# Gated linear attention plus a squared-ReLU MLP on one core: the first four chunks of x and w1 are loaded, split and multiplied in another arrangement

## The chip, the cores and the metric

One NeuronCore of a Trainium2 chip runs the whole kernel in one launch. The metric is device time in microseconds (us), the median over several runs; lower is better. One further execution was recorded by the hardware profiler, and every duration below comes from that recording.

## The reference

For x of 2048 x 448 the reference computes linear attention (branch a) and an MLP (branch b), mixed by a gate g for each row. It is cut to its core here:

```
x = A_x                                              # 1 x 2048 x 448
g = sigmoid((x * gate_w).sum(-1, keepdims=True))
# a: 16 heads of 28; phi(t) = where(t > 0, t + 1, exp(t)) + 1e-6
kv = einsum("bhsd,bhse->bhde", phi(k), v);  z = sum over s of phi(k)
a  = (phi(q) @ kv / (phi(q) . z + 1e-6)) @ wo
# b: 448 -> 1792 -> 448
h  = x @ w1 + b1
b  = relu(h)**2 @ w2 + b2
out = g * a + (1 - g) * b
```

All data are float32. The kernel keeps that precision by splitting each operand into a "hi" part, rounded to the format that TensorE multiplies (fp32r), and a "lo" part, the rest. A product is then three matmuls: hi by hi, lo of x by hi of w, hi of x by lo of w.

## The kernel before

The 2048 rows of x are four blocks of 512 columns of the transposed x (TB = 512). The 448 features are four chunks c of 128 partitions: chunks 0 to 2 are full, and chunk 3 holds the last 64 features twice, so that one matmul there does two of the three products. The 1792 hidden units are 14 tiles f of 128; seven of them make a half.

The program is one long list in a hand-written order; the order of the instructions on TensorE (PE), ScalarE (ACT) and VectorE (DVE) is that of the code. Loads are issued by SyncE (SP) through `load`, also in that order; a few transfers are issued by GpSimd (POOL).

The change touches the program's start. TensorE first runs 14 matmuls on constants (`warm_ps`). SyncE loads chunk 0 of x and of w1 in two transfers `xw` of 128 x 512, each with one half of both (`xw_raw[0]`, `xw_raw[1]`, in the profile `xwr`), and then chunks 1 to 3, x and w1 in turn, as six transfers of 256 KB with rows of 2 KB (`xr` and `w1r`). Each lands in a slot of a pool of 15 slots that the whole kernel goes round.

The splits follow. For chunk 0, ScalarE makes the hi part of x (`xh`) and VectorE that of w1 (`w`) for each half; TensorE multiplies the first two hidden tiles in halves of 256 columns (line 548), and VectorE makes the lo parts of x (`xl`), then of w1. For chunks 1 to 3, ScalarE makes hi of x, then hi of w1, and VectorE lo of x, then lo of w1 (`split_x`, `split_w1`, with `split_hi` on line 65 or 69, `split_lo` on line 72, and for chunk 3 of x `split_last` on lines 77 and 78). TensorE's matmuls of `up_chunk` (line 229) go term by term over the four tiles in chunk 0:

```
        if c == 0:
            for n in range(3):
                for f in range(0 if n else 2, 4):
                    up_chunk(first[f], 0, f, c, n)
        else:
            for f in range(4):
                up_chunk(first[f], 0, f, c)
```

In chunks 1 to 3 all three terms of one tile stand together, then those of the next. After chunk 3 come the keys of the first rows (`k_ps`, line 254), which need the split of `wk`, and the down product of tile 0 (`o_ps`, line 254), which needs `hh` and `hl`, the split of tile 0's squared ReLU (`hidden`). From there on the kernel goes in the same manner through all blocks.

Two further places matter. `hmask` is loaded into `hmr` by GpSimd in block 2 and split by ScalarE into `hm`. `queries` exchanges halves of 16 partitions for its chunk 3 (`swap`, line 475): four of the eight small transfers `qr<-qv` are issued by SyncE, four by GpSimd; VectorE adds the result in `join` (line 479).

Of the kernel before, what the change touches and what calls it, by code (L numbers as in the profile page):

```python
# [7 lines left out]
F = mybir.dt.float32  # L8
# [5 lines left out]
S, D, FF, H = 2048, 448, 1792, 16  # L14
DH = D // H
P = 128
TB = 512
NB = S // TB
NT = S // P
# [8 lines left out]


@with_exitstack  # L30
def gated_mix_kernel(ctx: ExitStack, tc: tile.TileContext, xw, xt, xn, wk, wq, wv, wo, w1a, w1b, w2, b1, b2, gw,
                     hmask, kvmask, halves, out):
    nc = tc.nc
    act, dve, pool, pe, sp = nc.scalar, nc.vector, nc.gpsimd, nc.tensor, nc.sync

    keep = ctx.enter_context(tc.tile_pool(name="keep", bufs=1))
# [11 lines left out]
    def bank(name):  # L48
        turn[0] ^= 1
        return ms_p.tile([P, 512], F, name=name, tag=f"ms{turn[0]}")  # L50
# [6 lines left out]
    def load(dst, src):  # L57
        sp.dma_start(out=dst, in_=src)  # L58
# [4 lines left out]
    def split_hi(eng, hi, src):  # L63
        if eng is act:
            act.activation(hi, src, AF.Copy)  # L65
        elif eng is pool:
            pool.tensor_scalar(hi, src, 1.0, 0.0, op0=ALU.mult, op1=ALU.add)
        else:
            eng.tensor_copy(hi, src)  # L69

    def split_lo(eng, lo, src, hi):
        eng.tensor_tensor(lo, src, f32(hi), op=ALU.subtract)  # L72
# [29 lines left out]
    x_raw, xs = {}, {}  # L102

    def load_x(b, c):
        x_raw[b, c] = slot([P, TB], F, f"xr{b}_{c}")
        load(x_raw[b, c], xt[b, c])
# [22 lines left out]
    w1_s, w1_raw = {}, {}  # L129

    def load_w1(h, g, c):
        w1_raw[h, g, c] = slot([P, (TB, 3 * P)[g]], F, f"w1r{h}{g}{c}")
        load(w1_raw[h, g, c], (w1a, w1b)[g][h, c])

    def new_w1(h, g):
        n, a, z = ((TB, 0, 16), (3 * P, 48, 0))[g]
        w = keep.tile([P, a + 7 * n + z], R, name=f"w1_{h}{g}", tag=f"w1{g}", bufs=1)
        w1_s[h, g] = w[:, a:a + 7 * n].rearrange("p (c n) -> p c n", c=7)
        return w1_s[h, g]
# [30 lines left out]
    ctx.enter_context(tc.manual_schedule(engines={pe.engine, act.engine, dve.engine}))  # L170


    part = [keep.tile([P, D], F, name=f"part{t}") for t in range(NT)]
    warm = nc.const_aps.tensor(1.0, (P, 256), mybir.dt.bfloat16)
    warm_ps = acc_p.tile([P, 512], F, name="warm_ps", tag="acc")
    for _ in range(14):
# [7 lines left out]
    xw_raw = []  # L184
    for n in range(2):
        xw_raw.append(slot([P, TB], F, f"xwr{n}"))
        load(xw_raw[n], xw[n])
    for c in range(1, 4):
        load_x(0, c)
        load_w1(0, 0, c)  # L190
    b1_s = keep.tile([P, NF], F, name="b1_s")
    half = keep.tile([P, 2], F, name="half")
    ones = keep.tile([P, 2], F, name="ones")
# [24 lines left out]
    def up_chunk(ps, b, f, c, only=None):  # L218
        h, fl = divmod(f, NH)
        g, i = divmod(fl, 4)  # L220
        w, cols = w1_s[h, g], slice(i * P, (i + 1) * P)
        xh, xl = xs[b]
        if c < 3:
            terms = [(w[:, c, cols], xh[:, c]), (w[:, c, cols], xl[:, c]), (w[:, 4 + c, cols], xh[:, c])]
        else:
            terms = [(w[:, 3, cols], xh[:, 3]), (w[:, 3, cols], xl[:, 3])]
        for n, (a, m) in enumerate(terms):
            if only in (None, n):
                pe.matmul(ps, a, m, start=(c == 0 and n == 0), stop=(c == 3 and n == 1))  # L229
# [219 lines left out]
    def queries(b, c):  # L449
        ps = bank(f"q_ps{b}_{c}")  # L450
        xh, xl = xs[b]
        cols = slice(c * P, (c + 1) * P)
        if c < 3:
            products(ps, terms_w(xh, xl, wq_s, cols))
        else:
            products(ps, [(wq_s[:, i, cols], x[:, i]) for i in range(4) for x in ((xh, xl) if i < 3 else (xh,))])
        e = slot([P, TB], F, f"qe{b}_{c}")
        r = slot([P, TB], F, f"qr{b}_{c}")
        v = slot([P, TB], F, f"qv{b}") if c == 3 else None
        pq[b, c] = e  # L460

        def after():
            phi(ps if c < 3 else v, e, r, e)
            if (b, "s") not in den:
                den[b, "s"] = slot([P, TB], F, f"ds{b}")
                dve.tensor_scalar(den[b, "s"], e, zc[:, c:c + 1], None, op0=ALU.mult)
            else:
                dve.scalar_tensor_tensor(den[b, "s"], e, zc[:, c:c + 1], den[b, "s"], op0=ALU.mult, op1=ALU.add)

        def swap():  # L470

            act.copy(v, ps)  # L472
            for p in range(0, P, 32):
                load(r[p:p + 16], v[p + 16:p + 32])
                pool.dma_start(out=r[p + 16:p + 32], in_=v[p:p + 16])  # L475
            return [join]

        def join():
            dve.tensor_tensor(v, v, r, op=ALU.add)
            after()  # L480
        return [swap if c == 3 else after]
# [53 lines left out]

    first = [mm_p.tile([P, 512], F, name=f"h_ps0_{f}", tag="mm") if f < 2 else bank(f"h_ps0_{f}") for f in range(4)]
    for c in range(4):
        if c == 0:  # L540
            xs[0] = new_x(0)
            w, (xh, xl) = new_w1(0, 0), [x[:, 0] for x in xs[0]]
            sides = slice(0, TB // 2), slice(TB // 2, TB)
            for n, cols in enumerate(sides):
                split_hi(act, xh[:, cols], xw_raw[n][:, sides[0]])
                split_hi(dve, w[:, 0, cols], xw_raw[n][:, sides[1]])
                for f in range(2):
                    pe.matmul(first[f][:, cols], w[:, 0, f * P:(f + 1) * P], xh[:, cols], start=(n == 0), stop=False)  # L548
            for m, (lo, hi) in enumerate(((xl, xh), (w[:, 4], w[:, 0]))):
                for n, cols in enumerate(sides):  # L550
                    split_lo(dve, lo[:, cols], xw_raw[n][:, sides[m]], hi[:, cols])
        else:
            split_x(0, c)
            split_w1(0, 0, c)
        if c == 0:
            for n in range(3):
                for f in range(0 if n else 2, 4):
                    up_chunk(first[f], 0, f, c, n)
        else:
            for f in range(4):  # L560
                up_chunk(first[f], 0, f, c)
    split_w2(0)
    split_w2(1)
    wk_s = keep.tile([P, 7, D], R, name="wk_s", tag="wkm", bufs=1)
# [53 lines left out]
    for b in range(1, NB):  # L618
        for f in range(NH):
            leave = leaves[b][f]  # L620
            run_todo()
            up(b, f)
            if f == 0:
                down(b - 1, NH - 1)
                half_done(b - 1)
                if b == 1:
                    for c in range(1, 4):
                        todo += gram(0, c)
                        run_todo()
            else:  # L630
                down(b, f - 1, leave=leave)
            if f == 1:
                todo += late_keys
                run_todo()
            if f == 0:
                load_xn(4 * b)
            if f < 4:
                if f < 3:
                    load_xn(4 * b + f + 1)
                if f == 0 and leave:  # L640
                    late_keys = keys(4 * b, leave)
                else:
                    late_keys = []
                    todo += keys(4 * b + f)
            elif f < 6:
                todo += gram(b, f - 4)
            else:
                todo += gram(b, 2)
                run_todo()
                todo += gram(b, 3)  # L650
            if b + 1 < NB:
                if 1 <= f < 5:
                    load_x(b + 1, f - 1)
                if 3 <= f:
                    split_x(b + 1, f - 3)
            if b == 2:
                if f < 4:
                    load_wq(f)
                if 1 <= f < 5:
                    split_wq(f - 1)  # L660
                if f == 5:
                    raw = slot([P, P], F, "hmr")
                    pool.dma_start(out=raw, in_=hmask)
                    split_hi(act, hm, raw)
                    load(half, halves)
            if b == 3:
                if f < 4:
                    load_w1(1, 0, f)
                if f == 4:
                    for c in range(4):  # L670
                        split_w1(1, 0, c)
                if f >= 2:
                    load_w2(NH + f - 2)
                if f >= 3:
                    split_w2(NH + f - 3)
                if f == 5:
                    key_sums()
                if f >= 5:
                    load_kv(2 * f - 10)
                    load_kv(2 * f - 9)  # L680
# [5 lines left out]
    for n, b in enumerate(order):  # L686
        then = order[n + 1] if n + 1 < NB else None
        for f in range(NF - NH, NF):
# [46 lines left out]
            if n == 0:  # L735
# [4 lines left out]
                if fl == 0:  # L740
                    for c in range(4):
                        load_w1(1, 1, c)
                    raw = kv_product()
# [29 lines left out]
    last, t = order[-1], 4 * order[-1] + 3  # L773
# [67 lines left out]
```

## Time and profile before

| | us |
|---|---|
| median of 3 runs (434.93 to 435.53) | 435.01 |
| the profiled execution's own time | 434.59 |
| its span, first to last instruction | 432.8 |
| TensorE busy | 428.8 |
| VectorE busy | 284.9 |
| ScalarE busy | 174.6 |
| GpSimd busy | 72.1 |

The span is what the profile's rows divide up; the remaining 1.8 us of the execution's own time lie around it. Matmuls are pipelined, so a busy TensorE can still lose time: how far apart the matmuls start says more than the busy share.

### The profile page before, as it was taken

To read this page: it belongs to the slowest core of one execution; us is meant where nothing else is said; L and a number is where in the kernel's file an instruction comes from. 1 tells how busy PE (TensorE), PEld (TensorE's weight loads), DVE (VectorE), ACT (ScalarE), POOL (GpSimd) and SP (SyncE) were. 2 spreads that over 40 slices of the span, in tenths; PEclk is the share of its full clock that TensorE was granted. 3 is DMA by queue.
4 is the path that set the end of the run, shared out by engine and by line. 5 is a ranking of instruction groups with operands and counts; after the bars stand their busy time and mean duration, and the time that the engine had idled before them with its cause. 6 is when DMAs were issued, how large, how long until landed. Compare 5 with 4: busy or idle time off the path is not lost.

```text
span 432.8 us, 5574 instructions
## 1 busy us (share of the span) xinstructions
PE 428.8 (99%) x2058; PEld 380.7 (88%) x2058; DVE 284.9 (66%) x464; ACT 174.6 (40%) x302; POOL 72.1 (17%) x93
## 2 busy tenths in 40 slices
PE   9999999999999999999999999999999999999997
PEld 6889999898989899898898888988888888888986
DVE  5999518843499437884459777887653966457624
ACT  6865324521346133453145543444433534233421
POOL 0055006500065002540010441000100001000000
PEclk9999999999999999999999999999999999999999
DMA  8742302020231211223234321230101401002002
GB/s 284 239 134 63 96 0 71 24 68 2 69 87 64 69 45 48 65 58 110 63 115 149 72 63 38 61 123 0 26 0 44 141 0 27 0 0 86 0 2 85
DMA packets 18412, 29.11 MB, mean 67 GB/s; under 512 B 2897, under 2 KB 12737, under 8 KB 18385
## 3 DMA queue, kind: packets, MB, share of 16 engines
q1 hardware_dynamic: 16480, 26.46, 19.8%
q0 software_dynamic: 1760, 2.20, 2.3%
q8 instruction: 16, 0.26, 0.3%
q14 instruction: 12, 0.09, 0.1%
q10 hardware_dynamic: 144, 0.10, 0.1%
HBM read 22.43 MB, written 3.67 MB: 60 GB/s over the span
## 4 chain that ended last, share of the span: by engine, by line
PE 98%; DMA 1%; ACT 0%; DVE 0%; SPq 0%; issue 0%
PE h_ps L229 32%; PE o_ps L254 31%; PE q_ps L84 8%; PE a_ps L84 8%; PE g_ps L84 8%; PE k_ps L254 8%; PE kv_ps L404 1%; DMA xwr<-in_xw 1%; PE m_ps L84 1%; PE d_ps L84 0%; PE last L84 0%; PE z_ps L398 0%; PE h_ps L548 0%; ACT xh L65 0%; DVE last L785 0%; SPq L58 0%
## 5 line engine op out<-in xcount | busy, mean ns | idle before, releaser
L254 PE MATMUL o_ps<-w,hh 128*128 128x448 f32 x444 | 127.8, 362 | 0.0
L229 PE MATMUL h_ps<-xh,w 128*128 128x512 f32 x390 | 124.6, 390 | 0.0
L254 PEld LDWEIGHTS o_ps<-w,hh 128*128 128x128 f32 x444 | 83.2, 188 | 7.6
L229 PE MATMUL h_ps<-xl,w 128*128 128x512 f32 x224 | 86.7, 389 | 0.0
L229 PEld LDWEIGHTS h_ps<-xh,w 128*128 128x128 f32 x390 | 73.1, 188 | 14.7 <-DVE w L72 0.4
L254 PE MATMUL o_ps<-w,hl 128*128 128x448 f32 x222 | 80.4, 362 | 0.0
L233 ACT ACTIVATE hr<-h_ps,b_s 128x512 f32<-128x512 f32 x56 | 38.1, 680 | 85.9 <-PE h_ps L229 80.6
L69 DVE CAST hh<-hr 128x512 fp32r<-128x512 f32 x56 | 23.6, 421 | 61.4 <-ACT hr L234 61.3
L229 PEld LDWEIGHTS h_ps<-xl,w 128*128 128x128 f32 x224 | 42.0, 188 | 7.9
L254 PEld LDWEIGHTS o_ps<-w,hl 128*128 128x128 f32 x222 | 41.6, 188 | 3.7
L72 DVE TENSOR_TENSOR hl<-hr,hh 128x512 fp32r<-128x512 f32 x56 | 39.7, 709 | 3.3
L72 POOL TENSOR_TENSOR nl<-xnr,nh 128x384 fp32r<-128x384 f32 x16 | 17.2, 1075 | 119.0 <-ACT nh L65 118.9
L234 ACT ACTIVATE hr<-hr 128x512 f32<-128x512 f32 x56 | 35.4, 632 | 1.8
L84 PE MATMUL q_ps<-xh,wq_s 128*128 128x512 f32 x100 | 33.0, 389 | 0.0
L84 PE MATMUL a_ps<-m_s,qh 128*128 128x448 f32 x112 | 32.7, 362 | 0.0
L254 PE MATMUL k_ps<-wk_s,xh 128*128 128x448 f32 x112 | 32.7, 361 | 0.0
L475 POOL DMA_DIRECT2D qr<-qv x16 | 7.9, 505 | 124.2 <-ACT qv L472 94.4
L72 DVE TENSOR_TENSOR pl<-r,ph 128x448 fp32r<-128x448 f32 x16 | 23.7, 1482 | 0.0
L326 POOL TENSOR_TENSOR ksum<-ksum,r 128x448 f32<-128x448 f32 x15 | 23.3, 1557 | 1.1 <-DVE r L288 1.1
L84 PE MATMUL q_ps<-xl,wq_s 128*128 128x512 f32 x60 | 23.3, 389 | 0.0
L254 PE MATMUL k_ps<-wk_s,xl 128*128 128x448 f32 x64 | 23.2, 363 | 0.0
L84 PE MATMUL a_ps<-m_s,ql 128*128 128x448 f32 x64 | 23.2, 362 | 0.0
(118 smaller groups left out, 571.0 us busy)
## 6 DMA issues: line engine op xcount, KB each, us to landing
xr<-in_xt SPq DMA_DIRECT2D x27, 256.0 KB, 2.7
xnr<-in_xn SPq DMA_DIRECT2D x16, 224.0 KB, 2.6
out<-out SPq DMA_DIRECT2D x15, 224.0 KB, 1.9
w2r<-in_w SPq DMA_DIRECT2D x14, 224.0 KB, 2.8
w1r<-in_w1a SPq DMA_DIRECT2D x7, 256.0 KB, 2.8
w1r<-in_w1b SPq DMA_DIRECT2D x8, 192.0 KB, 3.4
m_s<-m POOLq DMA_DIRECT2D x12, 112.0 KB, 2.5
wqr<-in_wq SPq DMA_DIRECT2D x4, 256.0 KB, 2.7
```

What stands on the lines that cost most here:

```text
L69: eng.tensor_copy(hi, src)
L72: eng.tensor_tensor(lo, src, f32(hi), op=ALU.subtract)
L84: pe.matmul(out_ps, a, b, start=(i == 0), stop=(i == n - 1))
L229: pe.matmul(ps, a, m, start=(c == 0 and n == 0), stop=(c == 3 and n == 1))
L233: act.activation(r, ps, AF.Relu, bias=b1_s[:, f:f + 1])
L234: act.activation(r, r, AF.Square)
L254: pe.matmul(ps, a, m, start=start, stop=stop)
L326: pool.tensor_tensor(ksum, ksum, p, op=ALU.add)
L404: pe.matmul(kv_ps[:JE, js], wv_s[c][:, js], gsum[c][:, js], start=(c == 0), stop=(c == 3))
L475: pool.dma_start(out=r[p + 16:p + 32], in_=v[p:p + 16])
```

## The change

1. Chunks 1 to 3 of x and of the first 512 columns of w1 stand side by side in one input `xw4`. Each chunk is one transfer of 512 KB with rows of 4 KB. It lands in `sums`, one tile that later serves as the 16 tiles `part`; the six pool slots are no longer taken.
2. Chunk 0: VectorE makes the hi part of x, ScalarE that of w1, in tiles of 128 columns.
3. Chunk 1: VectorE makes the hi part of x, ScalarE that of w1. Chunks 2 and 3 are split as before.
4. Chunk 1's matmuls go term by term over the four tiles, as chunk 0's do.
5. In block 0's exchange, two of GpSimd's four transfers go to SyncE; `hmask` is loaded by SyncE.

```diff
-    part = [keep.tile([P, D], F, name=f"part{t}") for t in range(NT)]
+    sums = keep.tile([P, NT * D], F, name="sums")
+    part = [sums[:, t * D:(t + 1) * D] for t in range(NT)]
...
     for c in range(1, 4):
-        load_x(0, c)
-        load_w1(0, 0, c)
+        raw = sums[:, 2 * TB * (c - 1):2 * TB * c]
+        load(raw, xw4[c - 1])
+        x_raw[0, c], w1_raw[0, 0, c] = raw[:, :TB], raw[:, TB:]
...
-                pool.dma_start(out=r[p + 16:p + 32], in_=v[p:p + 16])
+                (sp if b == 0 and p < 64 else pool).dma_start(out=r[p + 16:p + 32], in_=v[p:p + 16])
...
             for n, cols in enumerate(sides):
-                split_hi(act, xh[:, cols], xw_raw[n][:, sides[0]])
-                split_hi(dve, w[:, 0, cols], xw_raw[n][:, sides[1]])
+                split_hi(dve, xh[:, 0, cols], xw_raw[n][:, sides[0]])
                 for f in range(2):
-                    pe.matmul(first[f][:, cols], w[:, 0, f * P:(f + 1) * P], xh[:, cols], start=(n == 0), stop=False)
+                    split_hi(act, w[:, 0, (2 * n + f) * P:(2 * n + f + 1) * P], xw_raw[n][:, (2 + f) * P:(3 + f) * P])
+                for f in range(2):
+                    pe.matmul(first[f][:, cols], w[:, 0, f * P:(f + 1) * P], xh[:, 0, cols], start=(n == 0), stop=False)
...
+        elif c == 1:
+            split_hi(dve, xh[:, c], x_raw[0, c])
+            split_hi(act, w[:, c], w1_raw[0, 0, c])
+            split_lo(dve, xl[:, c], x_raw[0, c], xh[:, c])
+            split_lo(dve, w[:, 4 + c], w1_raw[0, 0, c], w[:, c])
         else:
             split_x(0, c)
             split_w1(0, 0, c)
-        if c == 0:
-            for n in range(3):
-                for f in range(0 if n else 2, 4):
-                    up_chunk(first[f], 0, f, c, n)
-        else:
-            for f in range(4):
-                up_chunk(first[f], 0, f, c)
+        for n in range(3) if c < 2 else (None,):
+            for f in range(2 if (c, n) == (0, 0) else 0, 4):
+                up_chunk(first[f], 0, f, c, n)
...
-                    pool.dma_start(out=raw, in_=hmask)
+                    load(raw, hmask)
```

How the order of instructions moves is read from the two built programs. On TensorE, at the first matmuls of chunk 1, there stands before (`h_ps_0` to `h_ps_3` are the four hidden tiles; `xh`, `xl` and `w` as above, where `w` holds both hi and lo of w1):

```order
L229 MATMUL h_ps_0_165<-xh_169,w_00_171 128x512
L229 MATMUL h_ps_0_165<-xl_170,w_00_171 128x512
L229 MATMUL h_ps_0_165<-xh_169,w_00_171 128x512
L229 MATMUL h_ps_1_166<-xh_169,w_00_171 128x512
L229 MATMUL h_ps_1_166<-xl_170,w_00_171 128x512
L229 MATMUL h_ps_1_166<-xh_169,w_00_171 128x512
```

In the changed program, the same place of TensorE reads:

```order
L232 MATMUL h_ps_0_141<-xh_145,w_00_147 128x512
L232 MATMUL h_ps_1_142<-xh_145,w_00_147 128x512
L232 MATMUL h_ps_2_143<-xh_145,w_00_147 128x512
L232 MATMUL h_ps_3_144<-xh_145,w_00_147 128x512
L232 MATMUL h_ps_0_141<-xl_146,w_00_147 128x512
L232 MATMUL h_ps_1_142<-xl_146,w_00_147 128x512
L232 MATMUL h_ps_2_143<-xl_146,w_00_147 128x512
L232 MATMUL h_ps_3_144<-xl_146,w_00_147 128x512
L232 MATMUL h_ps_0_141<-xh_145,w_00_147 128x512
```

The lo part of x is asked for four matmuls after the chunk's first one, no longer one, and the lo part of w1 eight, no longer two.

On ScalarE, its first splits stand so before:

```order
L65 ACTIVATE xh_169<-xwr_110 128x256
L65 ACTIVATE xh_169<-xwr_112 128x256
L65 ACTIVATE xh_169<-xr_1_114 128x512
L65 ACTIVATE w_00_171<-w1r_116 128x512
L65 ACTIVATE xh_169<-xr_2_118 128x512
L65 ACTIVATE w_00_171<-w1r_120 128x512
L77 ACTIVATE xl_170<-xr_3_122,side 128x512
```

On ScalarE in the changed program (`sums` holds the raw chunks):

```order
L65 ACTIVATE w_00_147<-xwr_95 128x128 x2
L65 ACTIVATE w_00_147<-xwr_97 128x128 x2
L65 ACTIVATE w_00_147<-sums 128x512
L65 ACTIVATE xh_145<-sums 128x512
L65 ACTIVATE w_00_147<-sums 128x512
L77 ACTIVATE xl_146<-sums,side 128x512
```

Two splits of 256 columns became four of 128, and the hi part of chunk 1 of x left ScalarE; it stands on VectorE now, ahead of that chunk's two lo parts.

## Rows read from the trace of the kernel before

**Rows 1.** The page: busy time by engine, and the chain that ended last.

```profile
PE 428.8 (99%) x2058; PEld 380.7 (88%) x2058; DVE 284.9 (66%) x464; ACT 174.6 (40%) x302; POOL 72.1 (17%) x93
...
PE 98%; DMA 1%; ACT 0%; DVE 0%; SPq 0%; issue 0%
```

**Rows 2.** Timeline of matmuls: start us, us, engine, line, operation, tiles, count.

```profile
3.99 1.11 PE L548 MATMUL h_ps<-xh,w 128*128 128x256 f32 x4
4.94 0.63 PE L229 MATMUL h_ps<-xh,w 128*128 128x512 f32 x2
...
7.58 0.40 PE L229 MATMUL h_ps<-xl,w 128*128 128x512 f32 x1
...
13.09 0.39 PE L229 MATMUL h_ps<-xh,w 128*128 128x512 f32 x1
...
14.91 0.57 PE L254 MATMUL k_ps<-wk_s,xh 128*128 128x448 f32 x2
```

**Rows 3.** Timeline of weight loads (PEld); in brackets idle time and its releaser.

```profile
4.59 0.30 PEld L548 LDWEIGHTS h_ps<-xh,w 128*128 128x128 f32 x2 [0.28 <-ACT xh L65]
...
7.24 0.19 PEld L229 LDWEIGHTS h_ps<-xh,w 128*128 128x128 f32 x1 [0.29 <-ACT w L65]
...
7.97 0.30 PEld L229 LDWEIGHTS h_ps<-xh,w 128*128 128x128 f32 x2 [0.43 <-DVE w L72]
```

**Rows 4.** Timeline of ScalarE, then of VectorE, at the start.

```profile
4.12 0.42 ACT L65 ACTIVATE xh<-xwr 128x256 fp32r<-128x256 f32 x1 [0.19 <-DMA xwr<-in_xw]
5.90 0.63 ACT L65 ACTIVATE xh<-xr 128x512 fp32r<-128x512 f32 x1 [1.36 <-DMA xr<-in_xt]
6.56 0.63 ACT L65 ACTIVATE w<-w1r 128x512 fp32r<-128x512 f32 x1
...
4.13 0.29 DVE L69 CAST w<-xwr 128x256 fp32r<-128x256 f32 x1 [0.31 <-DMA xwr<-in_xw]
4.33 0.75 DVE L72 TENSOR_TENSOR xl<-xwr,xh 128x256 fp32r<-128x256 f32 x2
5.00 0.76 DVE L72 TENSOR_TENSOR w<-xwr,w 128x256 fp32r<-128x256 f32 x2
```

**Rows 5.** Groups by line and shape, ScalarE and VectorE: count, busy us, mean ns.

```profile
L65 ACT ACTIVATE hm<-hmr 128x128 fp32r<-128x128 f32 x1 | 0.3, 296 | 0.0
...
L69 DVE CAST hh<-hr 128x512 fp32r<-128x512 f32 x4 | 1.7, 427 | 0.3 <-ACT hr L234 0.2
```

**Rows 6.** Windows: us, busy by engine (count), PEclk, DMA share, GB/s.

```profile
4.50:5.00 0.50, 0.43 (x4) 0.41 (x4) 0.50 (x2) 0.04 (x1) 0.00 (x0) 1.00 0.92 176
5.00:5.50 0.50, 0.50 (x4) 0.41 (x4) 0.50 (x3) 0.00 (x0) 0.00 (x0) 1.00 0.75 287
7.00:7.50 0.50, 0.50 (x3) 0.26 (x2) 0.50 (x2) 0.50 (x2) 0.00 (x0) 1.00 1.05 406
...
15.00:60.00 45.00, 45.00 (x221) 41.06 (x220) 33.26 (x54) 23.26 (x44) 12.43 (x12) 1.00 0.33 95
```

**Rows 7.** Timelines of VectorE and of weight loads at the first down product.

```profile
15.60 0.69 DVE L72 TENSOR_TENSOR hl<-hr,hh 128x512 fp32r<-128x512 f32 x1
...
17.32 0.19 PEld L254 LDWEIGHTS o_ps<-w,hl 128*128 128x128 f32 x1
```

**Rows 8.** The moved transfers: the queries on tiles hmr and qv, and timelines.

```profile
L663 POOL DMA_DIRECT2D hmr<-in_hmask x1: 704/704/704, 139.0 to 139.0; - x1
L65 ACT ACTIVATE hm<-hmr x1: 296/296/296, 146.1 to 146.1; 128x128 fp32r<-128x128 f32 x1
...
133.69 0.33 SPq L58 DMA_DIRECT2D xr<-in_xt  x1
...
252.67 3.72 SPq L58 DMA_DIRECT2D qr<-qv  x4
...
262.60 0.69 DVE L479 TENSOR_TENSOR qv<-qv,qr 128x512 f32<-128x512 f32 x1
DMA to landing us min/median/max: 2.7/3.8/4.5
```

More of the change, by code (lines that the diff above doesn't have):

```diff
@@ L30, in gated_mix_kernel @@
 @with_exitstack
-def gated_mix_kernel(ctx: ExitStack, tc: tile.TileContext, xw, xt, xn, wk, wq, wv, wo, w1a, w1b, w2, b1, b2, gw,
+def gated_mix_kernel(ctx: ExitStack, tc: tile.TileContext, xw, xw4, xt, xn, wk, wq, wv, wo, w1a, w1b, w2, b1, b2, gw,
                      hmask, kvmask, halves, out):
@@ L541, in gated_mix_kernel @@
             xs[0] = new_x(0)
-            w, (xh, xl) = new_w1(0, 0), [x[:, 0] for x in xs[0]]
+            w, (xh, xl) = new_w1(0, 0), xs[0]
             sides = slice(0, TB // 2), slice(TB // 2, TB)
             for n, cols in enumerate(sides):
-                split_hi(act, xh[:, cols], xw_raw[n][:, sides[0]])
-                split_hi(dve, w[:, 0, cols], xw_raw[n][:, sides[1]])
+                split_hi(dve, xh[:, 0, cols], xw_raw[n][:, sides[0]])
                 for f in range(2):
-                    pe.matmul(first[f][:, cols], w[:, 0, f * P:(f + 1) * P], xh[:, cols], start=(n == 0), stop=False)
-            for m, (lo, hi) in enumerate(((xl, xh), (w[:, 4], w[:, 0]))):
+                    split_hi(act, w[:, 0, (2 * n + f) * P:(2 * n + f + 1) * P], xw_raw[n][:, (2 + f) * P:(3 + f) * P])
+                for f in range(2):
+                    pe.matmul(first[f][:, cols], w[:, 0, f * P:(f + 1) * P], xh[:, 0, cols], start=(n == 0), stop=False)
+            for m, (lo, hi) in enumerate(((xl[:, 0], xh[:, 0]), (w[:, 4], w[:, 0]))):
                 for n, cols in enumerate(sides):
                     split_lo(dve, lo[:, cols], xw_raw[n][:, sides[m]], hi[:, cols])
+        elif c == 1:
[3 more added lines that the diff above has]
+            split_lo(dve, w[:, 4 + c], w1_raw[0, 0, c], w[:, c])
         else:
@@ L815 @@
                         for n in range(2)]),
+        "xw4": np.concatenate([xt[0, 1:], w1[0, 1:, :, :TB]], axis=2),
         "xt": xt,
```

## The prediction

> **What bounds the kernel.** I read the page of the profile first: TensorE is busy 428.8 us, and the chain of waits is 98% TensorE [rows 1]. Then the windows: from 15 to 60 us TensorE works 45.00 of 45.00 us, at the full granted clock of 1.00 (2.4 GHz) [rows 6]. So only the work ahead of about 15 us can be won, where the timelines of matmuls and weight loads show waits. Eight 512-column matmuls lie between the starts at 13.09 and 14.91: (14.91 - 13.09) / 8 = 0.2275 us each when nothing waits [rows 2]. From the start at 4.94 to the first `k_ps` at 14.91 there are 42 of them (10 of chunk 0, 12 + 12 + 8 of chunks 1 to 3), which need 9.56; they take 9.97. So **0.41 us is lost in waits** behind 4.94. The weight loads show where: at 7.24 for ScalarE's hi part of w1, at 7.97 for VectorE's lo part [rows 3], both in chunk 1; the rest are the restarts behind them. Ahead of 4.94 there is the wait at 4.59 for ScalarE's hi part of x [rows 3].
>
> **Chunk 0: hi parts on exchanged engines.** The second half of `xw` is there at 4.12. ScalarE made its x part in 0.42, to 4.54, and the weight load followed at 4.59, 0.05 later [rows 3, 4]. VectorE takes 0.29 for as many columns, from 4.13 to 4.42 [rows 4], so the matmul can start at 4.47, and those at 4.94 move to 4.82: **0.12 gained**. The first half gains as much and no longer decides. Cover: ScalarE now makes w1's tiles of 128 columns, a shape whose duration only another tile shows, 0.30 [rows 5]. The two tiles of the second half are ready by 4.12 + 0.30 + 0.30 = 4.72 at the latest, and the second is asked for at 4.82 + 0.23 = 5.05; if it took 0.42 as 256 columns do, 4.96, still in time. VectorE's four lo parts keep their times, since they follow two casts of 256 columns as before: xl ready at 5.08 and asked for at 5.28, w1's at 5.76 and asked for at 6.19 [rows 4]. Chunk 0's last matmul is then followed at 4.82 + 10 x 0.2275 = 7.10.
>
> **Chunk 1: one transfer, split on two engines, matmuls by terms.** Before, ScalarE made hi of x at 5.90 and hi of w1 behind it at 6.56, in 0.63 each [rows 4]; now it makes only w1's, while VectorE casts x in 0.43 [rows 5]. The first matmul can start 0.63 + 0.05 after the landing. VectorE's xl comes 0.43 + 0.69 + 0.05 = 1.17 after the landing (0.69 is a lo part of 512 columns [rows 7]) and is asked for four matmuls, 0.91, after the first, that is 1.59 after the landing at the earliest; w1's lo comes by 1.91 and is asked for at 2.50. So both waits behind the chunk's first matmul go, and their cover is at least 0.4. What is left is the first matmul. It loses nothing when the 512 KB have landed by 7.10 - 0.68 = 6.42, or by 6.2 if its weight load is to be as far ahead as usual.
>
> When they land is not shown, since no load of that form is in this trace. Lower bound: `xw` was there at 4.12, and 524 kB at 406 GB/s take 1.29 [rows 6], so 5.41. Upper bound: the same bytes were both there at 6.56 [rows 4]. Between them lies a slack of the queues of 176 and 287 GB/s from 4.50 to 5.50 [rows 6], whose cause the rows don't tell. I take the middle, about 6.0: seven tenths of the way from 5.41 to 6.56 lie below 6.2. Then all 0.41 is recovered. At the upper bound the first matmul starts at 7.24 as before and restarts with 0.11 lost (7.58 - 7.24 = 0.34 against 0.23 [rows 2, 3]): `k_ps` at 7.24 + 0.11 + 32 x 0.2275 = 14.63, a gain of 0.28 in all.
>
> The Trainium skill, DMA: Bandwidth & Descriptors, section Bandwidth, advises transfers of 1 MiB and gives 0.95 us for 64 KB and 6.15 us for 1 MB; read straight between these, my estimate is 2.0 for 256 KB and 3.4 for 512 KB. One transfer instead of two would by that save 0.6, so land at 5.96 and give the full 0.54. No run here shows that saving: parts of 256 KB landed 0.66 apart, which 406 GB/s fills without a pause [rows 4, 6].
>
> **Chunks 2 and 3.** They keep their order. At the latest they land 1.29 and 2.58 after the upper bound, 7.85 and 9.14. ScalarE's two hi parts of chunk 2 then end at 7.85 + 2 x 0.63 = 9.11, and TensorE asks for them at 7.10 + 12 x 0.2275 = 9.83; its lo of x is ready at 9.17 + 0.05 and its lo of w1 at about 9.9, asked for at 10.06 and 10.28. Chunk 3 takes one ScalarE step and three VectorE steps: 9.14 + 0.63 + 3 x 0.69 = 11.84, an estimate from these rows, against 12.56. No cost.
>
> **The rest.** The six pool slots set free let later loads go out sooner, and `sums` takes its part sums long after the raw chunks were split; TensorE waits for none of them, as its full window shows [rows 6]. `hmask` was issued at 139.0 and used at 146.1; SyncE's last issue ahead of it was at 133.69, so it is free, and a landing after 4.5, the longest that rows 8 show, still leaves 2.6 [rows 8]. In block 0's exchange SyncE issues six transfers in place of four from 252.67 on. Four took 3.72, so six end by about 3.72 x 6 / 4 = 5.6 later, at 258.3; with the longest landing of 4.5 counted from an issue's start, about 0.9 ahead of that end (3.72 / 4), the last is there by 261.9, and VectorE adds at 262.60 [rows 8]. Without that cover VectorE's queue would stand still, with the next hidden tile's split behind it. GpSimd saves two issues ahead of nothing that TensorE waits for. All this at zero.
>
> **Sum.** 0.12 + 0.41 = 0.53 to 0.54 gained. The profiled execution gives 434.59 - 0.54 = 434.05; it lies 0.42 under the median of the runs shown, so against that median I forecast 435.01 - 0.54, **434.5 us**. The gain reaches the end if nothing behind needs TensorE late. The nearest cover is tile 0's `hl`, ready at 15.60 + 0.69 = 16.29 and loaded at 17.32 [rows 7]: of 1.03 there stay 0.49.
>
> **Rivals.**
> - **The pair lands when its second part did.** The x part was usable at 5.90, 0.66 before the w1 part [rows 4]; one transfer makes x wait for both. For it: the slack of 4.50 to 5.50 would lie in the same place. Gain 0.28: 434.7. The Trainium skill, DMA: Bandwidth & Descriptors, section Why a DMA increments its semaphore by 16 and not by 1, says that only the full count, of all engines, tells that the data are there; the trace agrees in that ScalarE's start on each part came separately.
> - **The gain is returned at the first down product.** VectorE has one split of 0.43 more in chunk 1; if it and a late third transfer make VectorE more than 0.49 later at `hl`, TensorE waits there. Against: VectorE starts x itself and doesn't wait 0.63 for ScalarE. Price up to the whole 0.54: 435.0.
> - **Slower.** The transfer for chunk 1 lands late as a whole, because half of it meets the slack and nothing may start until the rest is there. From a landing at 6.84 the gain of 0.28 is gone, and every tenth behind that costs a tenth; from 7.71 the kernel is slower by 0.87, 435.9 or more. Against: no more bytes stand ahead of it than before.
> - **Faster than the sum.** If `xw` itself lands earlier, because less traffic stands behind it, TensorE's start moves as a whole. 0.33 of that with the 0.54 gives 434.1. Against: the two `xw` transfers and what is ahead of them don't change.
>
> **Chances.** About 0.2%, 0.87 us, is what a measurement of this kernel can tell from no change. The forecast has 0.58 (its own range 434.3 to 434.7), the late pair 0.20, the returned gain 0.06, slower 0.06, faster than the sum 0.10. The first three, 0.84, are within 0.2%; faster is 0.10 and slower 0.06. The range that should hold 8 in 10 goes from 434.0 to 435.3.
>
> **What would show it.** In the changed profile: the first weight load of the second half of chunk 0 at about 4.47; chunk 1's first matmul at 7.1 to 7.24; no weight load waiting for a lo part of w1; `k_ps` at 14.4 (14.6 in the first rival); `hl` loaded without a wait near 16.8; windows from 15 us on full. I am wrong if the first `k_ps` is later than 14.7, if TensorE waits behind 15 us, or if a matmul of chunk 2 or 3 waits for a landing.

## The result, and the profile after

The kernel lost 0.55 us: 435.51 us median (434.49 to 436.29, 22 runs) against 434.96 of the kernel before, measured beside it (22 runs), ratio 1.0013 with a 95% interval of 1.0007 to 1.0019. The forecast was 434.5, with a range of 434.0 to 435.3. The profiled execution took 435.55 us, its span 433.8.

The loss stands in one place. Timeline of the changed kernel's matmuls (columns as in [rows 2]; in brackets idle time and its releaser):

```profile
4.02 1.01 PE L553 MATMUL h_ps<-xh,w 128*128 128x256 f32 x4
4.87 0.63 PE L232 MATMUL h_ps<-xh,w 128*128 128x512 f32 x2
...
6.26 1.08 PE L232 MATMUL h_ps<-xh,w 128*128 128x512 f32 x4
8.48 1.20 PE L232 MATMUL h_ps<-xh,w 128*128 128x512 f32 x4 [1.15 <-ACT w L65]
9.52 1.08 PE L232 MATMUL h_ps<-xl,w 128*128 128x512 f32 x4
10.44 1.30 PE L232 MATMUL h_ps<-xh,w 128*128 128x512 f32 x5
...
15.88 0.57 PE L257 MATMUL k_ps<-wk_s,xh 128*128 128x448 f32 x2
```

Chunk 0's last four matmuls start at 6.26, so the next could start at 6.26 + 4 x 0.2275 = 7.17. It starts at 8.48: 1.31 lost, and 0.13 more in the restart (9.52 - 8.48 = 1.04 for four matmuls, against 0.91). From 9.52 on 28 matmuls take 6.36, that is 0.227 each: nothing waits any more. `k_ps` stands at 15.88, 0.97 later than in [rows 2], and the span is 1.0 longer.

Timelines of the changed kernel for the weight load of chunk 0's second half, ScalarE and VectorE (answers to [rows 3, 4]):

```profile
4.52 0.30 PEld L553 LDWEIGHTS h_ps<-xh,w 128*128 128x128 f32 x2 [0.19 <-DVE xh L69]
...
3.58 1.11 ACT L65 ACTIVATE w<-xwr 128x128 fp32r<-128x128 f32 x4 [1.55 <-DMA xwr<-in_xw]
7.80 0.63 ACT L65 ACTIVATE w<-sums 128x512 fp32r<-128x512 f32 x1 [3.11 <-DMA sums<-in_xw]
9.06 0.63 ACT L65 ACTIVATE xh<-sums 128x512 fp32r<-128x512 f32 x1 [0.63 <-DMA sums<-in_xw]
...
4.18 0.29 DVE L69 CAST xh<-xwr 128x256 fp32r<-128x256 f32 x1 [0.31 <-DMA xwr<-in_xw]
7.80 0.43 DVE L69 CAST xh<-sums 128x512 fp32r<-128x512 f32 x1 [1.99 <-DMA sums<-in_xw]
```

Both engines start on chunk 1 at the same 7.80, when its transfer lands; before, ScalarE had x at 5.90 and w1 at 6.56 [rows 4]. The windows (answers to [rows 6]) show fewer bytes from 5.00 to 6.00 than before, and TensorE full from 15 us on, as before:

```profile
5.00:5.50 0.50, 0.50 (x4) 0.37 (x3) 0.50 (x3) 0.00 (x0) 0.00 (x0) 1.00 0.71 197
5.50:6.00 0.50, 0.50 (x3) 0.40 (x3) 0.31 (x1) 0.00 (x0) 0.00 (x0) 1.00 0.69 205
...
15.00:60.00 45.00, 45.00 (x220) 40.96 (x219) 34.68 (x58) 23.74 (x44) 12.51 (x12) 1.00 0.37 99
```

In the kernel before, the second of these windows reads:

```profile
5.50:6.00 0.50, 0.50 (x4) 0.42 (x3) 0.26 (x1) 0.10 (x1) 0.00 (x0) 1.00 1.05 402
```

### The profile page after: what moved, and what is told of

It reads as the page before. It is cut to its first block, busy times and chain, and to the rows that moved or that the text cites. A ratio compares the mean times of both kernels' runs of the same rounds, so it can differ in the third digit from the quotient of the medians.

```text
span 433.8 us, 5566 instructions
## 1 busy us (share of the span) xinstructions
PE 428.7 (99%) x2058; PEld 380.7 (88%) x2058; DVE 284.9 (66%) x465; ACT 173.5 (40%) x303; POOL 70.7 (16%) x90
## 3 DMA queue, kind: packets, MB, share of 16 engines
HBM read 22.43 MB, written 3.67 MB: 60 GB/s over the span
## 4 chain that ended last, share of the span: by engine, by line
PE 97%; DMA 1%; SPq 0%; ACT 0%; DVE 0%; issue 0%
PE h_ps L232 32%; PE o_ps L257 31%; PE q_ps L84 8%; PE a_ps L84 8%; PE g_ps L84 8%; PE k_ps L257 8%; DMA sums<-in_xw 1%; PE kv_ps L407 1%; PE m_ps L84 1%; PE d_ps L84 0%; PE last L84 0%; SPq L58 0%; PE z_ps L401 0%; ACT w L65 0%; DVE last L791 0%
```

## The experiments

Medians are of 11 runs each (e2 of 6, e17 of 5, e5 of 4); the kernel before had 435.00, 435.00, 435.05, 435.00 and 434.82 in the five series, 15 to 33 runs each. e11 and e12 are single executions and stand in the text. A chunk is called usable at the start of the first engine that waits for it; the beat is the distance between the starts of two matmuls.

| run | us | ratio to before, 95% interval |
|---|---|---|
| e1_two_loads | 434.96 | 0.9998 [0.9989, 1.0007] |
| e4_same_input | 435.06 | 0.9998 [0.9989, 1.0007] |
| e3_rows_2k | 435.74 | 1.0013 [1.0004, 1.0022] |
| e5_rest_later | 443.69 | 1.0201 [1.0185, 1.0217] |
| e2_merge_only | 437.12 | 1.0053 [1.0035, 1.0071] |
| e6_merge_1 | 435.59 | 1.0018 [1.0008, 1.0029] |
| e7_merge_23 | 435.03 | 1.0000 [0.9991, 1.0008] |
| e8_warm16 | 434.82 | 0.9996 [0.9987, 1.0005] |
| e9_before_warm16 | 434.91 | 0.9997 [0.9988, 1.0005] |
| e10_w1_first | 434.88 | 1.0002 [0.9993, 1.0011] |
| e13_splits_alone | 434.86 | 0.9995 [0.9986, 1.0003] |
| e14_splits_warm16 | 434.94 | 0.9998 [0.9989, 1.0007] |
| e15_moves_alone | 435.25 | 1.0008 [0.9999, 1.0017] |
| e16_w1_first_moved_back | 434.80 | 0.9992 [0.9983, 1.0000] |
| e17_by_rows | 437.19 | 1.0056 [1.0043, 1.0069] |
| e18_four | 436.06 | 1.0022 [1.0013, 1.0032] |

### Is it the merge, the rows, the input, or the traffic behind?

The first four kernels start from the changed one. **e1**:

```diff
-        load(raw, xw4[c - 1])
+        load(raw[:, :TB], xt[0, c])
+        load(raw[:, TB:], w1a[0, c])
```

> The changed kernel with chunks 1 to 3 loaded as before, x and w1 apart in transfers of 256 KB with rows of 2 KB from their own inputs; the other parts of the change stay. Three theories of the wait of 1.3 us ahead of chunk 1 in the changed kernel, where its 512 KB were usable only at 7.80. One landing: a single transfer counts only when its slowest share is there, so x and w1 both wait for it; parted, x is usable near 5.9 and w1 near 6.56 as before, chunk 1's first matmul starts at 7.1 to 7.3, the first k_ps near 14.5, and the kernel takes 0.4 to 0.5 us less than before the change, about 434.5. Long rows: the same here, since the rows are 2 KB again. Crowd behind (the loads of w2 and wk, which the change issues earlier, slow chunk 1): the same here, since eight transfers stand ahead of b1 again. So this run tells only whether the merged transfer is the cause at all; if the wait of 1.3 us stays, all three fall and the exchanged engines are to blame.

434.96: the loss is gone, but none of the forecast gain appears. **e4** cuts the two halves out of the new input, which tells the input from the transfer's size:

```diff
-        load(raw, xw4[c - 1])
+        load(raw[:, :TB], xw4[c - 1, :, :TB])
+        load(raw[:, TB:], xw4[c - 1, :, TB:])
```

> The changed kernel with chunks 1 to 3 as two transfers of 256 KB each, rows of 2 KB, both cut from the new joint input. Against the run with separate inputs this differs only in which input is read. One landing, long rows and crowd behind all say: as with separate inputs, x near 5.9, w1 near 6.5, total about 434.5. If the place of the data in memory (a new input read for the first time) were what holds the queues up between 4.5 and 6.5, this run would be as late as the changed kernel, chunk 1 usable near 7.8, about 435.5.

435.06, as e1: the input is not it. **e3** keeps one transfer but in pieces of 2 KB (`xw4` stacked instead of side by side):

```diff
-        load(raw, xw4[c - 1])
+        load(raw.rearrange("p (k t) -> p k t", k=2), xw4[c - 1].rearrange("k p t -> p k t"))
```

> The changed kernel with each of chunks 1 to 3 in one transfer of 512 KB as changed, but each row as two pieces of 2 KB (256 pieces in place of 128 rows of 4 KB). Long rows: the landing of chunk 1 comes back to about 6.5, k_ps near 14.6, total about 0.3 us under that of before, 434.7. One landing: nothing changes against the changed kernel, chunk 1 usable near 7.8, total about 435.5, a ratio of 1.001 to 1.002. Crowd behind: as one landing, 435.5.

435.74, the same loss: rows of 4 KB are not it. Its one profiled run was its fastest (434.31) and shows the forecast's case; here are its rows of ScalarE and of the first `k_ps`:

```profile
6.34 0.63 ACT L65 ACTIVATE w<-sums 128x512 fp32r<-128x512 f32 x1 [1.74 <-DMA sums<-in_xw]
...
14.38 0.57 PE L257 MATMUL k_ps<-wk_s,xh 128*128 128x448 f32 x2
```

With the landing at 6.34, under the 6.42 that the prediction asked for, `k_ps` comes at 14.38, what its sum gives (7.10 + 32 x 0.2275); that it fits to the hundredth is luck, since chunk 0 ended 0.03 earlier and one restart cost 0.06. So the arithmetic from the landing to `k_ps` holds. The gain did not all reach the end: in this profile TensorE loses 0.25 again in the first `o_ps`, as in e7 below, and the run took 0.28 less than the first profile of the kernel before, not 0.54. Of e3's 11 runs 9 took more than 435.1. **e5** holds back what is loaded after `b1`, by four loads of 1 KB ahead of `w2`:

```diff
+    pad = rest.tile([P, 8], F, name="pad")
+    for i in range(4):
+        load(pad[:, 2 * i:2 * i + 2], halves)
```

> The changed kernel with four transfers of 1 KB each put behind b1, so that the loads of w2 and wk are issued only after chunk 1 has landed. Crowd behind: chunk 1 is usable by about 6.3, k_ps near 14.4, total about 434.6, unless w2 and wk then come too late for the keys. One landing and long rows: chunk 1 stays near 7.8, and the total at 435.5 or up to 0.5 above it, as w2 and wk come later.

Chunk 1 was usable at 8.50, later still, so the loads of `w2` and `wk` behind it are not what holds it up. The 8.2 us over the changed kernel lie elsewhere: some 2 at the first `k_ps` and `o_ps`, where `w2` and `wk` are late now and TensorE waits for their splits, and the most of it spread evenly from 28 us to the end, where the matmuls' beat is longer (the starts of `o_ps` 0.205 apart on the mean, against 0.201). The new tile `pad` moves other tiles in memory; that this is the reason was not tried, so e5 answers only the question of the landing. **e2** is the kernel before with the merge alone:

```diff
-        load_x(0, c)
-        load_w1(0, 0, c)
+        raw = sums[:, 2 * TB * (c - 1):2 * TB * c]
+        load(raw, xw4[c - 1])
+        x_raw[0, c], w1_raw[0, 0, c] = raw[:, :TB], raw[:, TB:]
```

> The kernel before with one part of the change alone: chunks 1 to 3 of x and w1 in one transfer of 512 KB each. Theory M (one landing costs what two of half the size don't, because x may not start before the slowest share of the 512 KB is there): slower than before by 0.5 us or more, since here ScalarE makes x's and w1's hi parts one behind the other after the landing (1.26 in place of 0.63), about 435.6 to 436.2. Rival (the loss comes from the other parts, the exchange of hi parts or the order by terms, and is set off by the two transfers): about 435.0.

437.12: the merge alone costs 2.1 us. ScalarE's and TensorE's rows of its profile:

```profile
8.46 0.63 ACT L65 ACTIVATE xh<-sums 128x512 fp32r<-128x512 f32 x1 [4.08 <-DMA sums<-in_xw]
8.99 0.61 ACT L65 ACTIVATE w<-sums 128x512 fp32r<-128x512 f32 x1
...
9.66 0.51 PE L231 MATMUL h_ps<-xh,w 128*128 128x512 f32 x1 [1.68 <-ACT w L65]
```

Behind a landing at 8.46 two hi parts follow one another on ScalarE, and the first matmul stands 1.20 behind the landing; in the changed kernel it is 8.48 - 7.80 = 0.68. So the split on two engines does its work: it accounts for 0.52 of the 1.50 by which `k_ps` comes later here (17.38) than in the changed kernel. 0.66 of the rest is the later landing of this execution; whether the merge alone lands later as a rule was not tried. **e6** and **e7** merge chunk 1 alone, and chunks 2 and 3 alone (e7: `c > 1`):

```diff
-        load(raw, xw4[c - 1])
+        if c == 1:
+            load(raw, xw4[c - 1])
+        else:
+            load(raw[:, :TB], xt[0, c])
+            load(raw[:, TB:], w1a[0, c])
```

> The changed kernel, with chunk 1 alone in one transfer of 512 KB; chunks 2 and 3 as x and w1 apart, 256 KB each. Theory M (the cost is the late landing of the chunk that TensorE asks for first): as the changed kernel, about 435.5. Rival (the cost lies in the longer row of large transfers as a whole, chunks 2 and 3 crowding chunk 1): about 435.0, as with six transfers.

> The changed kernel, with chunk 1 as x and w1 apart, 256 KB each, and chunks 2 and 3 in one transfer of 512 KB each. Theory M: chunks 2 and 3 are asked for 2.7 and 5.5 us later than chunk 1, so their one landing costs nothing: about 435.0 or a little less, as with six transfers. Rival (crowding): about 435.5, as the changed kernel.

435.59 and 435.03: the loss goes with chunk 1's transfer (the two programs end alike, 3.67 and 3.74 behind the last matmul's start). ScalarE in e6, then in e7:

```profile
7.80 0.63 ACT L65 ACTIVATE w<-sums 128x512 fp32r<-128x512 f32 x1 [3.21 <-DMA sums<-in_xw]
```

```profile
6.96 0.63 ACT L65 ACTIVATE w<-sums 128x512 fp32r<-128x512 f32 x1 [2.31 <-DMA sums<-in_w1a]
8.96 0.63 ACT L65 ACTIVATE xh<-sums 128x512 fp32r<-128x512 f32 x1 [1.37 <-DMA sums<-in_xw]
```

In e7 chunk 2 waits for its merged transfer too, until 8.96, and this costs nothing in the median. Its profile, of its slowest run (435.75), shows a cost all the same. Its weight loads:

```profile
10.98 0.30 PEld L236 LDWEIGHTS h_ps<-xh,w 128*128 128x128 f32 x2 [0.28 <-DVE w L72]
...
17.90 0.19 PEld L261 LDWEIGHTS o_ps<-w,hl 128*128 128x128 f32 x1 [0.28 <-DVE hl L72]
...
19.50 0.30 PEld L261 LDWEIGHTS o_ps<-w,hh 128*128 128x128 f32 x2 [0.29 <-DVE r L294]
```

VectorE starts on chunk 2 late, and TensorE waits for its lo part of w1 and then at the first down products: 0.41 is lost behind `k_ps`. In the seven kernels with all of chunks 1 to 3 in two transfers (e1, e4, e8, e10, e13, e14, e16) nothing is.

### What makes the one transfer late?

**e11** is the changed kernel, profiled once more:

> The changed kernel once more, for a second look at the landing of chunk 1. In its first look the 512 KB were usable at 7.80; in kernels that differ from it in the rows or in what is loaded later, at 6.34 and 8.50. Theory M (the landing of one transfer of this size spreads by a microsecond or more from run to run): another moment between 6.3 and 8.5, and the first k_ps about 8.1 behind it, or at 14.4 if it is there by 6.4. Rival (the moment belongs to the program): 7.8 again, within 0.1.

```profile
7.71 0.63 ACT L65 ACTIVATE w<-sums 128x512 fp32r<-128x512 f32 x1 [3.08 <-DMA sums<-in_xw]
...
15.78 0.57 PE L257 MATMUL k_ps<-wk_s,xh 128*128 128x448 f32 x2
```

435.48 us, and 7.71: the rival's side, nearly the first profile. Over the profiles chunk 1 in one transfer was usable at 7.80, 7.71, 7.80 (e6), 8.46 (e2), 8.50 (e5) and 6.34 (e3, other rows). The second of two transfers was there at 7.09 (e1), 6.37 (e4), 6.96 (e7), 6.46 (e8, e16), 6.59 (e10), 6.16 (e13) and 7.06 (e14), though it carries the last of the same bytes; in the old arrangement w1's hi part started at 6.56 (before), 6.60 (e9), 6.97 (e12) and 7.06 (e15). So two transfers spread too, over 0.9 us, and in five profiles of six the one transfer was later than all of them. A transfer reports its landing in 16 shares, and the trace's landing events of the changed kernel say how it is late: 12 are in by 5.49 and 15 by 6.37; the last comes at 7.78. In e11 two are late, at 7.54 and 7.69.

**e17** and **e18** ask whether size or form decides, both on e13 below. e17 halves each chunk by partitions, e18 takes chunk 1 in four pieces and chunks 2 and 3 in one each:

```diff
-        load(raw[:, :TB], xt[0, c])
-        load(raw[:, TB:], w1a[0, c])
+        load(raw[:64], xw4[c - 1, :64])
+        load(raw[64:], xw4[c - 1, 64:])
```

```diff
+            for n in range(4):
+                load(raw[:, n * TB // 2:(n + 1) * TB // 2], xw4[0, :, n * TB // 2:(n + 1) * TB // 2])
```

> Parts 2 to 4 with chunks 1 to 3 as two transfers of 256 KB each, cut not between x and w1 but between partitions 0 to 63 and 64 to 127, with rows of 4 KB: x's hi part needs both, as with one transfer. SyncE's count is that of the kernel before. Theory S (a transfer of 512 KB ends late by itself; two of 256 KB end earlier whatever they hold): chunk 1 usable at 6.2 to 7.1, and 434.9 as with x and w1 apart. Rival (the gain of two transfers is that x can start before w1 is there): 435.2 or more. A third (rows of 4 KB are late in either): 435.5.

> Parts 2 to 4 with chunk 1 as four transfers of 128 KB with rows of 1 KB, chunks 2 and 3 as one each; SyncE's count is that of the kernel before. Theory S, carried on: smaller pieces land no later, chunk 1 usable at 6.5 or earlier, 434.6 to 434.9. Rival (from 256 KB down SyncE's issues, about 0.45 each, and short rows cost what the pieces give): last piece usable at 7 or later, 435.0 to 435.3.

437.19 and 436.06: theory S is not borne out, smaller transfers are not early by themselves. One window of e17, then ScalarE of e18:

```profile
7.00:7.50 0.50, 0.33 (x2) 0.00 (x0) 0.00 (x0) 0.00 (x0) 0.00 (x0) 1.00 0.96 221
```

```profile
7.39 0.63 ACT L65 ACTIVATE w<-sums 128x512 fp32r<-128x512 f32 x1 [2.73 <-DMA sums<-in_xw]
```

Over 64 partitions the DMA engines are as busy (0.96) and move 221 GB/s in that window, where the kernel before moved 406 [rows 6]; chunk 1 is usable at 8.05, and chunk 3 is late too. So e17 changed the rate along with the size and can't tell them apart. In e18 the fourth piece has 15 shares in by 6.38 and the last at 7.30: a last share is late in a small piece too. Not all of e18's 1.2 us over the kernel before is chunk 1's: merged chunk 2 was usable at 9.72, and TensorE waits for it and again at the first `o_ps`, as in e7. Why one share trails, and why two transfers by x and w1 mostly escape it, no run here shows; it stays open.

### Where the forecast gain went: the start

**e12** is the kernel before, profiled once more (434.99 us):

> The kernel before once more, for a second look at its start. In the first look the 0.23 us beat of 512-column matmuls set in with the first of them, and 0.41 us was lost in waits behind 4.94. Theory K (the rise to 2.4 GHz comes later in many runs, and then chunk 0 ends later and the waits at chunk 1 are hidden behind it): if the beat is 0.43 at 5 us, fewer waits in chunk 1 and yet a later k_ps, 15.0 to 15.3. Rival (the start is always the same): k_ps at 14.9 with the same waits.

```profile
5.17 0.73 PE L229 MATMUL h_ps<-xh,w 128*128 128x512 f32 x2
...
15.32 0.57 PE L254 MATMUL k_ps<-wk_s,xh 128*128 128x448 f32 x2
```

Its weight loads at chunk 1, and ScalarE's hi part of w1:

```profile
7.66 0.19 PEld L229 LDWEIGHTS h_ps<-xh,w 128*128 128x128 f32 x1 [0.35 <-ACT w L65]
...
8.38 0.30 PEld L229 LDWEIGHTS h_ps<-xh,w 128*128 128x128 f32 x2 [0.43 <-DVE w L72]
...
6.97 0.63 ACT L65 ACTIVATE w<-w1r 128x512 fp32r<-128x512 f32 x1 [0.46 <-DMA w1r<-in_w1a]
```

`k_ps` comes at 15.32, 0.41 later than in the first profile, and 15.88 - 15.32 = 0.56 is the loss that the medians show. The first profile, on which the sum was built, was an early one. From the first `k_ps` to the last matmul's start the program takes 414.6 in every profile but those of e3, e5, e7, e17 and e18, so a run's time follows from its `k_ps` and its end; by that sum, an estimate, a run at the median has its `k_ps` at 15.3 in the kernel before.

The start isn't the same in each run, for two reasons: chunk 1's w1 was usable at 6.97 here, and TensorE's clock, read from the beat, rises at another moment (its first two 512-column matmuls start 0.34 apart, not 0.23). The waits, though, are the same two. Behind chunk 0's last matmul the old arrangement loses 0.41 (before), 0.47 (e12), 0.54 (e9) and 0.99 (e15) to `k_ps`; the seven kernels with parts 2 to 4 and two transfers for each chunk lose 0 to 0.15. **e8** and **e9** lengthen the row of constants, in e1 and in the kernel before:

```diff
-    for _ in range(14):
+    for _ in range(16):
```

> Two transfers of 256 KB for each of chunks 1 to 3, the rest of the change kept, and 16 instead of 14 matmuls on constants ahead of chunk 0. In the profiles so far the 512-column matmuls of chunk 0 begin 0.43 us apart and come to 0.23 at a moment that differs by run: 3.8 to 4.1 us in three profiles, 5.2, 5.9 and 6.5 in three others. Theory K (TensorE's idle stretches between the constants and chunk 0's halves put the rise to 2.4 GHz off, and a late rise eats the gain of the other parts): with the stretches filled the rise is near 4 in this run and the median falls by 0.2 to 0.5, to 434.5 to 434.8. Rival (the moment does not depend on these stretches): 435.0, or up to 0.2 more since chunk 0 starts behind two more matmuls.

> The kernel before with 16 instead of 14 matmuls on constants, nothing else. Theory K (a late rise to 2.4 GHz costs time at the start of every kernel of this family): the kernel before gains by them too, 0.2 to 0.4, to about 434.7. Rival (the two matmuls don't move the median): 435.0. If it gains as much as the two-transfer kernel did (434.82), the difference that the rest of the change makes is below 0.2 in either.

**e10** also loads chunk 1's w1 first:

```diff
+        pair = [(raw[:, :TB], xt[0, c]), (raw[:, TB:], w1a[0, c])]
+        for dst, src in pair[::-1] if c == 1 else pair:
+            load(dst, src)
```

> The two-transfer kernel with 16 matmuls on constants, and in chunk 1 w1's transfer ahead of x's. In the profile of that kernel x was usable at 5.70 and w1 at 6.46; ScalarE needs 0.63 for w1's hi part and VectorE 0.43 for x's, so the order decides: with x first the first matmul of chunk 1 stands 0.68 behind the second landing, with w1 first 0.48. Theory W (a wait of 0.1 and a restart of 0.11 are left there): 0.2 less, about 434.6. Rival (where the landing is early enough, or chunk 0 ends late for the clock, nothing waits): 434.8.

434.82, 434.91 and 434.88: no effect that these intervals tell from none.

### Where the forecast gain went: the end

**e13** is parts 2 to 4 of the change alone: e1 with part 5 undone.

```diff
-                (sp if b == 0 and p < 64 else pool).dma_start(out=r[p + 16:p + 32], in_=v[p:p + 16])
+                pool.dma_start(out=r[p + 16:p + 32], in_=v[p:p + 16])
...
-                    load(raw, hmask)
+                    pool.dma_start(out=raw, in_=hmask)
```

(It is three transfers in all; "five" in the expectation miscounts them.)

> Parts 2 to 4 of the change alone: exchanged hi parts and chunk 1 by terms; x and w1 of chunks 1 to 3 as six transfers of 256 KB, the exchange's transfers and hmask on GpSimd as before. From the last matmul's start to the end of the span the profiles show 3.31 to 3.33 in both looks at the kernel before, in the changed kernel, and in the variant with one transfer and rows of 2 KB; 3.64 to 3.66 in the kernels that have six transfers and the five moved ones at once (three more issues by SyncE), 3.67 with two more, 3.74 with one more, 3.49 with three fewer. Theory E (the end of the program depends on how many transfers SyncE has issued, and 0.33 of what the two-transfer kernel gained at the start went there): with the old count the end is 3.31 again and the median 434.96 - 0.33, about 434.6. Rival (those 0.33 are chance, or belong to the new order at the start): an end of 3.6 and 435.0.

**e14** and **e16** undo part 5 in e8 and e10 by the same lines; **e15** makes the opposite edit in the kernel before.

> The same with 16 instead of 14 matmuls on constants. Theory E: 434.82 - 0.33 = 434.5, with an end of 3.31 behind the last matmul's start and k_ps near 14.5. Rival: 434.8.

> The kernel before with part 5 alone: two of GpSimd's four exchange transfers of block 0 and hmask issued by SyncE, three issues more. Theory E: nothing else moves, k_ps as before, and the end behind the last matmul's start is 3.64 in place of 3.31, so the median is about 435.3. Rival (the end does not depend on the count): 435.0.

> Parts 2 to 4 alone, 16 matmuls on constants, and in chunk 1 w1's transfer ahead of x's. Theory E: 434.88 - 0.33, about 434.5, with an end of 3.31. Rival: 434.9.

The last output's issue on ScalarE's queue and the span, in e13 and then in e15:

```profile
core 0 of [0], span 432.2 us
...
429.64 0.37 ACTq L793 DMA_DIRECT2D out<-last  x1
```

```profile
core 0 of [0], span 433.6 us
...
430.75 0.37 ACTq L786 DMA_DIRECT2D out<-last  x1
```

The program ends 432.2 - 429.64 = 2.6 behind that issue in e13, and 433.6 - 430.75 = 2.9 in e15; from the last matmul's start it is 3.32 and 3.65. So theory E's mechanism holds in each of the four: the count of SyncE's transfers sets the end. SyncE's semaphore events at the end say how. Its transfers go round eight DMA semaphores, and it waits for these in a fixed order. In the kernel before the wait for the last landing is the last of them; with three transfers more (e8) five waits follow it, about 0.06 each, with one more (e7) seven, with three fewer (e2) three. So it is not a price for each transfer: it is the place of the last one in the row of eight. In the medians it is worth 0.25 in e15 (435.25, an interval that just reaches none) and about 0.1 between e1 and e13, less than the 0.33 expected; in e14 nothing, against the 0.3 expected.

e13 and e14 differ in two matmuls on constants, and their profiles show how far the start can move. First e13, then e14:

```profile
4.74 0.63 PE L233 MATMUL h_ps<-xh,w 128*128 128x512 f32 x2
5.20 1.08 PE L233 MATMUL h_ps<-xl,w 128*128 128x512 f32 x4
...
14.30 0.57 PE L258 MATMUL k_ps<-wk_s,xh 128*128 128x448 f32 x2
```

```profile
5.05 1.05 PE L233 MATMUL h_ps<-xh,w 128*128 128x512 f32 x2
5.91 1.37 PE L233 MATMUL h_ps<-xl,w 128*128 128x512 f32 x4
...
15.30 0.57 PE L258 MATMUL k_ps<-wk_s,xh 128*128 128x448 f32 x2
```

In e13 two matmuls start 5.20 - 4.74 = 0.46 apart, 0.23 each; in e14 5.91 - 5.05 = 0.86, 0.43 each. 512 columns in 0.43 us are 1.2 columns a ns, which is the lower of the clock's two levels (1.2 and 2.4 GHz); the granted clock in the windows' rows is 1.00 in both, so the level is read from the beat alone. Neither waits for chunk 1, and yet the first `k_ps` stands 1.00 apart, and the runs took 433.98 and 434.98. That the two extra matmuls would bring the rise forward falls with e14.

A late rise can thus cost more than the whole forecast gain. That it is what takes the gain back in a run at the median is not shown. By the sum above a median run of e13 has its `k_ps` near 15.2, between these two profiles, and e13's profile is of its fastest run. A beat of 0.42 to 0.43 for two matmuls or more was seen in 3 of the 15 profiles with chunk 0's new split (e1, e5, e14). The other candidate is w1's landing, at 7.09 and 7.06 in e1 and e14, where the sum needs 6.42. Over e13, e14 and e16 together the median is 434.86 (33 runs) against 435.00 (33 runs).

## Why the prediction was wrong

- **The step that failed** is "when they land". I took 6.0 for chunk 1's 512 KB, between 5.41 and 6.56; it was 7.80 and 7.71. The upper end was no bound: it held that the same bytes can't land later in one transfer than in two, and it was one execution's moment; in e12 and e15 even the two transfers of the old arrangement were there only at 6.97 and 7.06. The lower one came from a rate, and a landing is set by the last share, not by the rate: 15 of 16 were in by 6.37, under my 6.42. The Trainium skill, DMA: Bandwidth & Descriptors, section Bandwidth, made it 5.96 by my estimate; the measurement decides against it here (its figures are of transfers issued from GpSimd, these were issued by SyncE).
- **The rival "Slower"** is what happened, with its price: 0.87 from a landing at 7.71, that is `k_ps` at 15.78, and e11 shows both numbers. The time that it named, 435.9, is 0.4 above the median, because it too was counted from the early first profile. Its chance of 0.06 was too low, and it was weighed as if the bytes ahead of the transfer were all that counts.
- **Chunk 0**: the mechanism was right. The weight load stood at 4.18 + 0.29 + 0.05 = 4.52; with `xw` 0.06 later than in the kernel before the gain was 0.07 (4.94 to 4.87), not 0.12. In e11, with `xw` at the same 4.12, the weight load stood at 4.47 and the matmul at 4.81, as forecast.
- **Chunk 1's covers**: right. Its first matmul stood 0.68 behind the landing, and no load of a lo part waited.
- **Chunks 2 and 3 without cost**: right by luck. Chunk 2 landed near 9.06, past my latest 7.85, and cost nothing only because TensorE was late itself. With chunk 1 in two transfers (e7) it landed at 8.96, and TensorE waited in chunk 2 and again at `hl`.
- **The rest at zero**: right in the sum, for a reason that I didn't see. Part 5 alone gives three SyncE transfers more and a longer end (e15), the merge three fewer and an end of 3.49 (e2); together the count is the old one, and the end is 3.31 as before.
- **The 0.41**: right as a wait, wrong as a gain. The waits stand in all four profiles of the old arrangement (0.41 to 0.99) and go with parts 2 to 4 (0 to 0.15). But parts 2 to 4 alone (e13) gave 0.14 in the median, inside an interval that reaches none, and 0.61 only in the profile with an early rise (434.59 - 433.98). I took one early start as if every run began so; what takes back the rest in a run at the median stays open.
- **The return at `hl`**, the other rival, didn't occur in the changed kernel, which was late itself: TensorE loads `hl` without a wait. Where chunk 1 was earlier and chunks 2 and 3 were merged it did: 0.41 in e7, 0.25 in e3. So even with the landing that I forecast the sum was too large by about 0.25.

The best that was found, e16, has 434.80, ratio 0.9992 [0.9983, 1.0000]: an interval that just reaches none.

## What to carry to other kernels

A transfer that the critical engine asks for first is as late as its last share; keep the first one in the pieces that are asked for, and merge later ones only where there is slack up to their last user: merged chunks 2 and 3 cost nothing in e7's median, yet in its profile TensorE waited behind them. A wait at the start, seen in one execution, is worth what its removal gives in the median of several: profile the start more than once before it goes into a sum. When the number of transfers of a queue changes, read the end of the program as well as the place of the edit.

## What was not expected of the hardware

- The moment of the rise from 1.2 to 2.4 GHz behind the same 14 or 16 matmuls on constants: by the beat of the matmuls it was there before 4.8 in e13, and not until 5.9 or later in e14. The windows' PEclk column shows 1.00 in both, so no row but the beat shows the rise.
- The end of the program depends on how many transfers SyncE issued: 3.31 from the last matmul's start with the old count, 3.49 with three fewer, 3.64 with three more, 3.67 with two more, 3.74 with one more. The order follows the place of the last transfer in the row of eight semaphores.
- Transfers over 64 of 128 partitions moved 221 GB/s in a window with the DMA engines 0.96 busy (e17).
